# Linear attention, SwiGLU and a bilinear layer in one kernel: attention's stores move to ScalarE's queue, four weight tiles are staged whole, and the gated product stays in PSUM

## The chip, the cores and the metric

The kernel runs on one core of a Trainium2 chip. The metric is the device time of one execution in microseconds; the number of a kernel is the median of its runs. Besides, one execution is profiled, and all durations below come from it.

## What is computed

Three layers in fp32, each feeding the next. Attention works on 4 batches with 8 heads, 576 positions and a head dimension of 64; the other two layers work on its 4 * 576 = 2304 tokens, with a model width of 512 and a hidden width of 1536:

```
q_s = exp(q - max over d);   q_s = q_s / (sum over d + 1e-9)
k_s = exp(k - max over s);   k_s = k_s / (sum over s + 1e-9)
x   = q_s @ (k_s^T @ v)                    per batch and head
x   = (silu(x @ w_gate) * (x @ w_val)) @ moe_w_out
out = ((x @ w_a) * (x @ w_b)) @ moe2_w_out
```

## The kernel before, in words

**Tokens and weights.** The tokens are cut into five token tiles: 512 positions of each of the four batches, and a last tile of 256 columns with the 64 positions that remain of each batch. The hidden width is cut into 12 weight tiles of 128 (f = 0 to 11). A weight tile holds its share of the three matrices of a layer, and each matrix twice: as a high part in fp32r and as what remains (the low part). A product of two fp32 numbers is made of three matmuls with these parts, so a token tile of 512 columns takes 12 matmuls for the gate, 12 for the value and 12 for the down product in each weight tile. The products of layer 0 go through the token tiles 0, 1, 2, the tile of the remainders, and 3 (`order`), then layer 1 goes through all five.

**Conversion of the weights** (`convert`, L308 to 374; `split`, L292 to 294). The raw halves of a weight tile are loaded in three DMAs of 256 KB (L331, L336) into a staging buffer `raw`. ScalarE takes the absolute value (L353; VectorE can do it at L355), scales the raw low words (L357), VectorE clamps, shifts and joins (L359, L362, L365), GpSimd adds (L370), ScalarE copies the high part into the weight tile (L293), and VectorE or GpSimd subtracts it to get the low part (`pair`, L287). Layer 0's weight tiles are converted while token tile 0 goes through them, layer 1's later. The staging buffers are `wr0` and `wr1`, and for the first ten tiles of layer 0 also `xraw`. Tile 0 is converted matrix by matrix, the others in two halves of all three matrices (`convert_tile`, L376). Each weight tile has its own place `w0` to `w11` in SBUF, which layer 0 and layer 1 share. The places `w8` to `w11` serve first as working memory of attention's units of batches 0 and 1.

**Attention** (`attend`) works in units of two heads, four units to a batch. The remainders' positions of batch 0 come in six loads of 64 KB (`load_rests`, L385). A unit ends with two products: 512 columns (`xt`, L589) and the 64 remaining ones (`xl`, L599). Batch 0's `xt` is split at once into the input of token tile 0 (`xhl`); of the other batches ScalarE copies it to `xs` (L596), and SyncE's queue stores it to a DRAM tensor `x` (L597). The remainders are copied to `xq` (L603) and stored (L604) for every batch. A later token tile is loaded from that tensor (`next_x`, L614).

**Gate and value** (`ups`, `gated`, `down`). Two PSUM banks, `gv0` and `gv1`, take the gate's and the value's products; either may go into either. ScalarE applies silu (layer 1: a copy) from the gate's bank to `s` in SBUF (L665), VectorE multiplies `s` by the value's bank into `s` (L668), ScalarE copies the high part to `h` (L293), and VectorE or GpSimd subtracts it from `s` to get h's low part (L287). The down product of tile f comes after the gate and value products of tile f + 1.

**What orders the work.** A planner (`Plan`) gets every operation with its engine, an estimated cost, the buffers that it reads and writes, and, for the products, a due time. `prepare` hands due times back from consumers to producers. `order` then simulates the engines and each time takes the ready operation that is due first on the engine that is free first; it also picks the place of each buffer that may have several, and the engine where there is a choice. A VectorE operation marked `port` and a GpSimd operation are never planned at the same time. `emit` issues the operations in that order, and each engine executes its own in order. Every load of weights and of q, k and v is chained to the one before (`load`, L303), so they issue on SyncE's queue in the order of the program; stores stand on the same queue. The planner reckons a DMA at a start of 1.1 us, an end of 0.95 us and `DMA_RATE` bytes per us.

Of the kernel before, what the change touches and what calls it, by code (L numbers as in the profile page):

```python
# [30 lines left out]
class Plan:  # L31
# [12 lines left out]
    DMA_START, DMA_END, DMA_RATE = 1.1, 0.95, 360e3  # L44
# [50 lines left out]
    def prepare(self):  # L95

        ops = self.ops
        self.succ = [[] for _ in ops]
        for n, op in enumerate(ops):
            for d in op["deps"] | op["order"]:  # L100
                self.succ[d].append(n)
        self.due = [0.0] * len(ops)
        for n in reversed(range(len(ops))):
            op = ops[n]
            cost = op["cost"]
            if op["engine"] == "sync":
                cost += self.DMA_START + self.DMA_END + op["nbytes"] / self.DMA_RATE
            t = self.FAR
            for s in self.succ[n]:
                hop = self.hop(op["engine"], ops[s]["engine"], self.SLACK) if n in ops[s]["deps"] else 0.0  # L110
                t = min(t, self.due[s] - hop)
            t -= cost
            self.due[n] = t if op["wanted"] is None else min(t, op["wanted"])

    def order(self):
# [34 lines left out]
        while len(done) < len(ops):  # L150
# [30 lines left out]
            if engine == "sync":  # L181
# [30 lines left out]
def kernel(  # L212
# [64 lines left out]
    def pool_us(n, streams=2):  # L277
        return (0, 0.14 + n / 1100, 0.15 + n / 449, 0.18 + n / 590)[streams]
# [17 lines left out]
    def dma(fn, nbytes, reads, writes, due=None, after=(), issue=0.475):  # L296
        return add("sync", issue, fn, reads, writes, due=due, nbytes=nbytes, after=after)
# [12 lines left out]
    RAW = WR + ("xraw",)  # L310
    TOP = 122880.0
    LEAST = 2.0 ** -15

    def convert(l, f, c, ms, c0, c1, spare):
# [4 lines left out]
        raw = Buf(sp, [P, n, width, 2], U32, RAW if spare else WR, f"wr{name}")  # L319
# [5 lines left out]
        parts = [(raw, x) for x in range(n)]  # L325
        for x, m in enumerate(ms):
            w_parts[l, f][m].append(c)

            def get(x=x, m=m):
                if m < 2:  # L330
                    nc.sync.dma_start(  # L331
                        out=raw()[:, x].rearrange("p (c n) t -> p c (n t)", n=P),
                        in_=mats[l][m][:, f * 2 * P:(f + 1) * 2 * P].rearrange(
                            "(c p) n -> p c n", p=P)[:, c0 // P:c1 // P, :])
                else:
                    nc.sync.dma_start(  # L336
                        out=raw()[:, x].rearrange("p n t -> p (n t)"),
                        in_=mats[l][m][f * P:(f + 1) * P, 2 * c0:2 * c1])

            load(get, P * width * 8, [(raw, x)])  # L340

        def low():
            return raw()[:, :, :, 0]

        def high():
            return raw()[:, :, :, 1]

        def part(t):
# [9 lines left out]
            out=low(), in_=low(), func=AF.Copy, scale=2.0 ** -29), parts, [(raw, "low")])  # L358
# [13 lines left out]
        add("gpsimd", pool_us(e), lambda: whole(nc.gpsimd), [a, (raw, "low")], [a],  # L372
# [3 lines left out]
    def convert_tile(l, f):  # L376
        for h in range(2):
            spare = l == 0 and f < NF - 2
            list(convert(l, f, h, [0, 1, 2], h * WC // 2, (h + 1) * WC // 2, spare))
# [5 lines left out]
    def load_rests(b, src, at):  # L385

        for h in range(HG):
            load(lambda h=h: nc.sync.dma_start(
                out=rests()[rest(h), at],
                in_=src[b, :, SM:S, :].rearrange("(g h) s d -> h s g d", h=HG)[h]),  # L390
                SL * KD * D * 8, [(rests, (at, h))], issue=0.65)

    def attend(b, g, xhl, due):
# [200 lines left out]
        else:  # L594
            ob = Buf(op, [P, 512], F32, ("ob0", "ob1"), f"xs{u}")
            add("scalar", act_us(SM), lambda: nc.scalar.copy(out=ob(), in_=px()), [px], [ob])  # L596
            dma(lambda: nc.sync.dma_start(out=xd[0][b]()[:, g, :], in_=ob()), P * SM * 4,  # L597
                [ob], [(xd[0][b], g)])
# [5 lines left out]
        dma(lambda: nc.sync.dma_start(out=xd[0][B]()[:, g, b * SL:(b + 1) * SL], in_=oc()[:, 0:SL]),  # L604
            P * SL * 8, [oc], [(xd[0][B], (g, b))])
# [55 lines left out]
    def gated(l, i, f, ga, gb):  # L661
# [7 lines left out]
            out=s()[:, 0:n], in0=s()[:, 0:n], in1=gb()[:, 0:n], op=ALU.mult), [s, gb], [s])  # L669
        split(lambda: h()[:, 0, 0:n], lambda: h()[:, 1, 0:n], lambda: s()[:, 0:n], n, (h, 0), (h, 1), s)  # L670
# [132 lines left out]
```

## Time and profile before

| | |
|---|---|
| median of 3 runs | 1038.8 us (1037.66 to 1039.71) |
| the profiled execution | 1037.9 us |
| its span, first to last instruction | 1036.0 us |
| TensorE busy (matmuls) | 977.9 us, 94% of the span |
| VectorE busy | 431.8 us, 42% |
| ScalarE busy | 357.7 us, 35% |
| GpSimd busy | 178.2 us, 17% |
| moved by DMA | 74.22 MB |

In the profile PE is TensorE's matmuls and PEld its weight loads, DVE is VectorE, ACT is ScalarE, POOL is GpSimd, SP is SyncE and SPq its queue of DMA issues. A time in a row counts from the start of the span. In a timeline a row has the start, the duration, the engine, the line, the operation and the tiles written and read; in brackets stands how long the engine was idle before it and what ended that. An operation's line can be that of a helper: L287 is every difference of a high and a low part and some of attention's, L293 every copy of a high part, so the tiles tell which it is.

### The profile page before, as it was taken

To read this page: it belongs to the slowest core of one execution; us is meant where nothing else is said; L and a number is where in the kernel's file an instruction comes from. 1 tells how busy PE (TensorE), PEld (TensorE's weight loads), DVE (VectorE), ACT (ScalarE), POOL (GpSimd) and SP (SyncE) were. 2 spreads that over 40 slices of the span, in tenths; PEclk is the share of its full clock that TensorE was granted. 3 is DMA by queue.
4 is the path that set the end of the run, shared out by engine and by line. 5 is a ranking of instruction groups with operands and counts; after the bars stand their busy time and mean duration, and the time that the engine had idled before them with its cause. 6 is when DMAs were issued, how large, how long until landed. Compare 5 with 4: busy or idle time off the path is not lost.

```text
span 1036.0 us, 12377 instructions
## 1 busy us (share of the span) xinstructions
PE 977.9 (94%) x4792; PEld 797.4 (77%) x4792; DVE 431.8 (42%) x758; ACT 357.7 (35%) x574; POOL 178.2 (17%) x156
## 2 busy tenths in 40 slices
PE   4777879999999999999999999999999999999997
PEld 3455656677778777799888788888888888888897
DVE  5876688633334333432665774131113112111211
ACT  4556565432334323422355543121112112111211
POOL 4543444301110101100145443000000000000000
PEclk9989989999999999999999999999999999999999
DMA  6445543311121111521133531020002000100100
GB/s 198 120 134 168 168 149 111 117 56 47 47 69 59 46 46 46 175 92 61 62 123 122 194 108 54 1 82 1 1 1 82 1 1 0 61 1 1 41 1 22
DMA packets 63876, 74.22 MB, mean 72 GB/s; under 512 B 12616, under 2 KB 51016, under 8 KB 62920
## 3 DMA queue, kind: packets, MB, share of 16 engines
q1 hardware_dynamic: 63816, 73.42, 22.4%
q8 instruction: 38, 0.62, 0.3%
q14 instruction: 22, 0.18, 0.1%
HBM read 60.29 MB, written 13.11 MB: 71 GB/s over the span
## 4 chain that ended last, share of the span: by engine, by line
PE 80%; DMA 6%; DVE 5%; SPq 3%; issue 2%; ACT 2%; POOL 2%; DVEq 0%; POOLq 0%; ACTq 0%
PE u L654 51%; PE acc L684 14%; PE acc L681 11%; DMA wr<-in_moe_w_out_dram 3%; PE kv L544 2%; POOL a L370 1%; DVE a L365 1%; SPq L331 1%; DVE h L287 1%; SPq L461 1%; PE xt L589 1%; PE kv L546 1%; PE qt L574 1%; DMA ut<-in_v_dram 1%; DMA x<-ob 1%
## 5 line engine op out<-in xcount | busy, mean ns | idle before, releaser
L654 PE MATMUL u<-xhl,w 128*128 128x512 f32 (+1 forms) x2856 | 621.9, 372 | 14.8 <-DVE w L287 12.6
L654 PEld LDWEIGHTS u<-xhl,w 128*128 128x128 f32 x2856 | 497.0, 189 | 110.6 <-DVE w L287 11.7
L668 DVE TENSOR_TENSOR s<-s,u 128x512 f32<-128x512 f32 (+1 forms) x120 | 76.1, 634 | 395.1 <-PE u L654 382.7
L681 PE MATMUL acc<-h,w 128*128 128x512 f32 (+1 forms) x720 | 167.6, 379 | 12.5 <-DVE h L287 10.7
L681 PEld LDWEIGHTS acc<-h,w 128*128 128x128 f32 x720 | 125.5, 190 | 42.3 <-DVE h L287 14.4
L684 PE MATMUL acc<-w,h 128*128 128x512 f32 x648 | 157.5, 391 | 0.1
L665 ACT ACTIVATE s<-u 128x512 f32<-128x512 f32 (+1 forms) x120 | 66.6, 555 | 262.0 <-PE u L654 255.2
L684 PEld LDWEIGHTS acc<-w,h 128*128 128x128 f32 x648 | 120.7, 188 | 26.2 <-DVE h L287 1.3
L293 ACT CAST h<-s 128x512 fp32r<-128x512 f32 (+1 forms) x120 | 69.1, 576 | 205.0 <-DVE s L668 204.7
L370 POOL TENSOR_TENSOR a<-a,wr 128x768 uint32<-128x768 uint32 (+1 forms) x49 | 99.4, 2033 | 205.0 <-DVE a L365 141.4
L287 DVE TENSOR_TENSOR h<-s,h 128x512 fp32r<-128x512 f32 (+1 forms) x119 | 84.3, 709 | 51.5 <-ACT h L293 51.3
L287 POOL TENSOR_TENSOR xhl<-xraw,xhl 128x512 fp32r<-128x512 f32 (+1 forms) x5 | 6.0, 1202 | 337.9 <-ACT xhl L293 240.9
L365 DVE SCALAR_TENSOR_TENSOR a<-wr,a 128x768 uint32<-128x768 uint32 (+1 forms) x49 | 52.4, 1077 | 0.5
L353 ACT ACTIVATE a<-wr 128x768 f32<-128x768 f32 (+1 forms) x38 | 33.7, 888 | 45.0 <-DMA wr<-in_moe_w_out_dram 34.9
L293 ACT CAST w<-a 128x768 fp32r<-128x768 f32 (+1 forms) x49 | 39.9, 818 | 23.2 <-POOL a L370 19.8
L357 ACT ACTIVATE wr<-wr 128x768 uint32<-128x768 uint32 (+1 forms) x49 | 43.8, 893 | 10.3 <-DMA wr<-in_moe_w_out_dram 10.3
L359 DVE TENSOR_SCALAR a<-a 128x768 f32<-128x768 f32 (+1 forms) x49 | 36.0, 739 | 18.8 <-ACT a L353 18.3
L287 DVE TENSOR_TENSOR w<-a,w 128x768 fp32r<-128x768 f32 (+1 forms) x38 | 38.3, 1021 | 8.5 <-ACT w L293 8.5
L567 POOL TENSOR_TENSOR ua<-ua,st 128x576 f32<-128x576 f32 x8 | 9.2, 1154 | 122.4 <-DVE st L566 122.4
L362 DVE TENSOR_SCALAR a<-a 128x768 uint32<-128x768 uint32 (+1 forms) x49 | 27.6, 572 | 0.8
L287 POOL TENSOR_TENSOR w<-a,w 128x768 fp32r<-128x768 f32 (+1 forms) x11 | 22.9, 2080 | 19.6 <-ACT w L293 19.6
L697 DVE COPY ob<-acc 128x512 f32<-128x512 f32 (+1 forms) x20 | 12.7, 636 | 27.9 <-DMA out_dram<-ob 19.9
(94 smaller groups left out, 439.2 us busy)
## 6 DMA issues: line engine op xcount, KB each, us to landing
wr<-in_moe_w_out_dram SPq DMA_DIRECT2D x46, 256.0 KB
xraw<-x SPq DMA_DIRECT2D x7, 1024.0 KB
wr<-in_moe_w_a_dram SPq DMA_DIRECT2D x24, 256.0 KB
wr<-in_moe_w_b_dram SPq DMA_DIRECT2D x24, 256.0 KB
wr<-in_moe_w_gate_dram SPq DMA_DIRECT2D x22, 256.0 KB
wr<-in_moe_w_val_dram SPq DMA_DIRECT2D x22, 256.0 KB
x<-ob SPq DMA_DIRECT2D x16, 256.0 KB
out_dram<-ob SPq DMA_DIRECT2D x16, 256.0 KB
```

What stands on the lines that cost most here:

```text
L287: engine.tensor_tensor(out=out(), in0=x(), in1=y(), op=op)
L293: add("scalar", act_us(n), lambda: nc.scalar.copy(out=hi(), in_=src()), [src_key], [hi_key])
L353: add("scalar", act_us(e) + 0.08, lambda: nc.scalar.activation(out=a().bitcast(F32), in_=high().bitcast(F32), func=AF.Abs), parts, [a], ot ...
L357: add("scalar", act_us(e) + 0.08, lambda: nc.scalar.activation(out=low(), in_=low(), func=AF.Copy, scale=2.0 ** -29), parts, [(raw, "low")])
L359: add("vector", dve_us(e, 2), lambda: nc.vector.tensor_scalar(out=a().bitcast(F32), in0=a().bitcast(F32), scalar1=TOP, scalar2=LEAST, op0= ...
L365: add("vector", dve_us(e), lambda: nc.vector.scalar_tensor_tensor(out=a(), in0=high(), scalar=0xC0000000, in1=a(), op0=ALU.bitwise_and, op ...
L370: engine.tensor_tensor(out=a(), in0=a(), in1=low(), op=ALU.add)
L654: nc.tensor.matmul(ps()[:, 0:n], lhsT=wv[:, c, :], rhs=x()[:, xs, c, 0:n], start=(a == 0 and c == 0), stop=(a == 2 and c == KD - 1))
L665: add("scalar", act_us(n), lambda: nc.scalar.activation(out=s()[:, 0:n], in_=ga()[:, 0:n], func=AF.Silu if l == 0 else AF.Copy), [ga], [s] ...
L668: add("vector", dve_us(n), lambda: nc.vector.tensor_tensor(out=s()[:, 0:n], in0=s()[:, 0:n], in1=gb()[:, 0:n], op=ALU.mult), [s, gb], [s])
L681: nc.tensor.matmul(ps()[:, 0:n], lhsT=w()[:, 4 + ws, o * P:(o + 1) * P], rhs=h()[:, hs, 0:n], start=begin, stop=end)
L684: nc.tensor.matmul(ps(), lhsT=h()[:, hs, o * P:(o + 1) * P], rhs=w()[:, 4 + ws, :], start=begin, stop=end)
```

## The change

The stores of `xs` and `xq` and the six loads of the remainders are issued from ScalarE's queue; the loads of the remainders leave the chain of loads. The raw words of layer 0's weight tiles 1 to 4 are staged whole, in the places `w4` to `w7`, which are not yet in use as weight tiles then; tile 0 and tiles 5 to 11 keep the small staging buffers. The multiplication of the gate writes its result into the value's PSUM bank and not into `s`, and both steps of the split read it there; the subtraction can no longer go to GpSimd and is not marked `port`. The planner reckons 300e3 bytes per us where it had 360e3, and takes an operation as a DMA by its bytes, not by its engine.

```diff
@@ -41,7 +41,7 @@
...
-    DMA_START, DMA_END, DMA_RATE = 1.1, 0.95, 360e3
+    DMA_START, DMA_END, DMA_RATE = 1.1, 0.95, 300e3
@@ -103,7 +103,7 @@
...
-            if op["engine"] == "sync":
+            if op["nbytes"]:
@@ -178,7 +178,7 @@
...
-            if engine == "sync":
+            if op["nbytes"]:
@@ -293,8 +293,8 @@
...
-    def dma(fn, nbytes, reads, writes, due=None, after=(), issue=0.475):
-        return add("sync", issue, fn, reads, writes, due=due, nbytes=nbytes, after=after)
+    def dma(fn, nbytes, reads, writes, due=None, after=(), issue=0.475, queue="sync"):
+        return add(queue, issue, fn, reads, writes, due=due, nbytes=nbytes, after=after)
@@ -308,42 +308,47 @@
...
+    AHEAD = 4
...
-    def convert(l, f, c, ms, c0, c1, spare):
+    def convert(l, f, c, ms, c0, c1, spare, raw=None):
...
-        raw = Buf(sp, [P, n, width, 2], U32, RAW if spare else WR, f"wr{name}")
+        if raw is None:
+            raw, rows, h = Buf(sp, [P, n, width, 2], U32, RAW if spare else WR, f"wr{name}"), (lambda: raw()), 0
+        else:
+            rows, h = (lambda: raw()[:, c]), c
...
-        parts = [(raw, x) for x in range(n)]
+        parts = [(raw, (h, x)) for x in range(n)]
...
             def get(x=x, m=m):
...
-                        out=raw()[:, x].rearrange("p (c n) t -> p c (n t)", n=P),
+                        out=rows()[:, x].rearrange("p (c n) t -> p c (n t)", n=P),
...
-                        out=raw()[:, x].rearrange("p n t -> p (n t)"),
+                        out=rows()[:, x].rearrange("p n t -> p (n t)"),
...
-            load(get, P * width * 8, [(raw, x)])
+            load(get, P * width * 8, [(raw, (h, x))])
         def low():
-            return raw()[:, :, :, 0]
+            return rows()[:, :, :, 0]
         def high():
-            return raw()[:, :, :, 1]
+            return rows()[:, :, :, 1]
@@ -355,7 +360,7 @@
...
-            out=low(), in_=low(), func=AF.Copy, scale=2.0 ** -29), parts, [(raw, "low")])
+            out=low(), in_=low(), func=AF.Copy, scale=2.0 ** -29), parts, [(raw, (h, "low"))])
@@ -369,14 +374,16 @@
         def whole(engine):
...
-        add("gpsimd", pool_us(e), lambda: whole(nc.gpsimd), [a, (raw, "low")], [a],
+        add("gpsimd", pool_us(e), lambda: whole(nc.gpsimd), [a, (raw, (h, "low"))], [a],
...
     def convert_tile(l, f):
+        spare, raw = l == 0 and f < NF - 2, None
+        if l == 0 and f <= AHEAD:
+            raw = Buf(wp, [P, 2, 3, WC // 2, 2], U32, f"w{f + NF - KD - AHEAD - 1}", f"wr{l}_{f}")
...
-            spare = l == 0 and f < NF - 2
-            list(convert(l, f, h, [0, 1, 2], h * WC // 2, (h + 1) * WC // 2, spare))
+            list(convert(l, f, h, [0, 1, 2], h * WC // 2, (h + 1) * WC // 2, spare, raw))
@@ -385,10 +392,10 @@
     def load_rests(b, src, at):
...
-            load(lambda h=h: nc.sync.dma_start(
+            dma(lambda h=h: nc.scalar.dma_start(
...
-                SL * KD * D * 8, [(rests, (at, h))], issue=0.65)
+                SL * KD * D * 8, [], [(rests, (at, h))], issue=0.65, queue="scalar")
@@ -594,15 +601,15 @@
...
-            dma(lambda: nc.sync.dma_start(out=xd[0][b]()[:, g, :], in_=ob()), P * SM * 4,
-                [ob], [(xd[0][b], g)])
+            dma(lambda: nc.scalar.dma_start(out=xd[0][b]()[:, g, :], in_=ob()), P * SM * 4,
+                [ob], [(xd[0][b], g)], queue="scalar")
...
-        dma(lambda: nc.sync.dma_start(out=xd[0][B]()[:, g, b * SL:(b + 1) * SL], in_=oc()[:, 0:SL]),
-            P * SL * 8, [oc], [(xd[0][B], (g, b))])
+        dma(lambda: nc.scalar.dma_start(out=xd[0][B]()[:, g, b * SL:(b + 1) * SL], in_=oc()[:, 0:SL]),
+            P * SL * 8, [oc], [(xd[0][B], (g, b))], queue="scalar")
@@ -666,8 +673,8 @@
...
-            out=s()[:, 0:n], in0=s()[:, 0:n], in1=gb()[:, 0:n], op=ALU.mult), [s, gb], [s])
-        split(lambda: h()[:, 0, 0:n], lambda: h()[:, 1, 0:n], lambda: s()[:, 0:n], n, (h, 0), (h, 1), s)
+            out=gb()[:, 0:n], in0=s()[:, 0:n], in1=gb()[:, 0:n], op=ALU.mult), [s, gb], [gb])
+        split(lambda: h()[:, 0, 0:n], lambda: h()[:, 1, 0:n], lambda: gb()[:, 0:n], n, (h, 0), (h, 1), gb, psum=True)
```

## Rows read from the trace of the kernel before

**Rows 1.** The stretches, 45 to 400 us: busy us (and instructions) of each engine, granted clock, DMA share, GB/s.

```profile
45.00:100.00 55.00, 41.03 (x174) 30.50 (x174) 41.33 (x67) 35.98 (x50) 23.49 (x18) 0.90 0.54 168
100.00:200.00 100.00, 85.95 (x393) 63.40 (x392) 77.42 (x128) 55.67 (x80) 41.44 (x31) 0.96 0.42 133
200.00:400.00 200.00, 200.00 (x985) 158.32 (x985) 70.37 (x164) 69.48 (x110) 18.06 (x33) 1.00 0.18 55
```

**Rows 2.** Groups by line, 45 to 200 us: busy us, mean ns | idle before, its releaser.

```profile
L287 DVE TENSOR_TENSOR h<-s,h 128x512 fp32r<-128x512 f32 x11 | 10.4, 942 | 0.7 <-ACT h L293 0.7
```

**Rows 3.** Instructions on tile h, 690 to 980 us: min/median/max ns, first and last start.

```profile
L287 DVE TENSOR_TENSOR h<-s,h x36: 692/693/1428, 692.4 to 975.5; 128x512 fp32r<-128x512 f32 x36
```

**Rows 4.** Waits of TensorE, 0 to 200 us: total us, times, longest.

```profile
PE u L654 <- DVE w L287: 12.6, 5, 7.5
PE acc L681 <- DVE h L287: 9.2, 5, 6.0
PE xt L589 <- ACT ut L583: 6.6, 4, 2.9
```

**Rows 5.** Timeline around 41 us.

```profile
41.23 0.89 ACT L353 ACTIVATE a<-wr 128x768 f32<-128x768 f32 x1 [4.26 <-DMA wr<-in_moe_w_out_dram]
...
43.17 1.96 PE L589 MATMUL xt<-ut 128*128 128x512 f32 x2 [2.77 <-ACT ut L583]
```

**Rows 6.** Timeline, 52 to 71 us.

```profile
52.53 1.83 POOL L370 TENSOR_TENSOR a<-a,wr 128x768 uint32<-128x768 uint32 x1 [0.72 <-DVE a L365]
...
56.46 0.69 DVE L519 TENSOR_REDUCE st<-ut 128x8 f32<-128x512 f32 x1 [3.42 <-DMA ut<-in_q_dram]
...
70.59 0.56 DVE L355 TENSOR_SCALAR a<-wr 128x768 uint32<-128x768 uint32 x1 [1.11 <-DMA wr<-in_moe_w_out_dram]
```

**Rows 7.** Waits of SyncE's queue, 100 to 130 us.

```profile
SPq L597 <- ACT xq L603: 6.0, 1, 6.0
```

**Rows 8.** Timeline, 122 to 132 us.

```profile
122.04 0.40 SPq L331 DMA_DIRECT2D wr<-in_moe_w_gate_dram  x1
...
127.84 0.89 ACT L353 ACTIVATE a<-wr 128x768 f32<-128x768 f32 x1 [4.66 <-DMA wr<-in_moe_w_out_dram]
...
128.76 0.56 DVE L359 TENSOR_SCALAR a<-a 128x768 f32<-128x768 f32 x1 [3.88 <-ACT a L353]
...
131.34 4.30 POOL L370 TENSOR_TENSOR a<-a,wr 128x768 uint32<-128x768 uint32 x2 [9.59 <-issue]
```

**Rows 9.** Instructions on tiles xs and xq, 45 to 200 us: min/median/max ns of an issue.

```profile
L597 SPq DMA_DIRECT2D x<-xs x4: 339/354/433, 87.5 to 183.7; - x4
...
L604 SPq DMA_DIRECT2D x<-xq x5: 338/377/2167, 59.6 to 186.4; - x5
```

**Rows 10.** Timeline of the opening.

```profile
2.27 1.41 SPq L388 DMA_DIRECT2D rests<-in_k_dram  x2
...
6.33 1.26 SPq L388 DMA_DIRECT2D rests<-in_v_dram  x2
...
9.04 0.66 ACT L353 ACTIVATE a<-wr 128x512 f32<-128x512 f32 x1 [7.02 <-DMA wr<-in_moe_w_gate_dram]
```

**Rows 11.** The chain that ended last, in order of time: start us, us, what.

```profile
9.47 6.12 DMA ut<-in_v_dram
```

**Rows 12.** The stretch 10 to 20 us, columns as in rows 1.

```profile
10.00:20.00 10.00, 4.18 (x25) 3.19 (x26) 6.99 (x22) 6.53 (x15) 4.27 (x7) 1.00 0.90 306
```

**Rows 13.** Line 668 in the whole span: min/median/max ns.

```profile
L668 DVE TENSOR_TENSOR s<-s,u x120: 414/689/690, 52.4 to 1027.7; 128x512 f32<-128x512 f32 x96, 128x256 f32<-128x256 f32 x24
```

**Rows 14.** Timeline in the full stretch, 693 to 697 us.

```profile
693.21 0.60 ACT L665 ACTIVATE s<-u 128x512 f32<-128x512 f32 x1 [0.82 <-DVE h L287]
...
695.30 0.69 DVE L668 TENSOR_TENSOR s<-s,u 128x512 f32<-128x512 f32 x1 [2.19 <-PE u L654]
...
696.68 0.69 DVE L287 TENSOR_TENSOR h<-s,h 128x512 fp32r<-128x512 f32 x1 [0.69 <-ACT h L293]
```

**Rows 15.** The chain that ended last, behind it.

```profile
697.95 5.44 PE u L654 x24
```

## The prediction, made before the changed kernel was built or run

> **What bounds the kernel now.** I read the stretches of the span first, then who TensorE waits for, then the timeline around the waits. The stretches [rows 1] show two regimes. From 200 us TensorE is busy all the time (200.00 of 200); an edit elsewhere can win nothing there unless it takes work from TensorE, and this change takes none. Before 200 us it is not: 41.03 of the 55 from 45 to 100, 85.95 of the next 100. That is most of the first pass over token tile 0, in which the weights are converted as they are used. In those 155 us (45 to 200) VectorE is busy 41.33 + 77.42 = 118.8 and GpSimd 23.49 + 41.44 = 64.9. Together that is more than 155, so the two must overlap, and GpSimd's sums and VectorE's two-input operations visibly get in each other's way: the first pass's subtraction for h takes 942 ns on average [rows 2], against a median of 693 late in the run, where GpSimd has little to do [rows 3]. So the first pass hangs on the conversion chain (load, ScalarE, VectorE, GpSimd, ScalarE, VectorE). TensorE's waits before 200 us [rows 4] agree: 12.6 us for converted weights, 9.2 us for the low half of h, which stands in VectorE's queue among conversions, 6.6 us for a ScalarE copy of attention. What a part of the change is worth is the idle time that it takes out of this chain; whatever ends the first pass earlier moves all that follows earlier by as much.
>
> **Tiles 1 to 4 staged whole.** The 24 loads of these tiles no longer wait for one of three small buffers, so they can issue right behind the opening loads. Three idle times before 100 us end with a load. (a) ScalarE stands 4.26 us for tile 1's first half, with attention's transposed q queued behind it, and TensorE waits 2.77 us for that copy [rows 5]. With tile 1 landed long before, the copy comes that much earlier: I take 2.8, between 0 (another conversion takes ScalarE's slot) and 4.3. (b) VectorE waits 3.42 us for batch 1's q, until 56.46 [rows 6]; GpSimd had stopped at 52.53 + 1.83 = 54.36, so both stood for 2.1. Those loads sit in SP's queue behind weight loads that waited for a buffer. I take 2.1, between 0 and 3.4. (c) VectorE waits 1.11 for weights at 70.59 [rows 6]: 1.1, between 0 and 1.1. Together **6.0, between 0 and 8.8**. What is late next is VectorE itself: TensorE's 12.6 us for weights are mostly its work and not the loads', so I count nothing more for them. From tile 5 on the ring has three buffers as before.
>
> **Attention's stores on ScalarE's queue.** SP works in order, and a store that waits for attention holds the weight loads behind it. The clear case: SP waits 6.0 us at the store of xs [rows 7]; the weights behind it issue at 122.04, ScalarE stands 4.66 us for them, VectorE 3.88, GpSimd has been idle for 9.59 by 131.34 [rows 8]. With the store gone the load could issue up to 6.0 us earlier, more than ScalarE waits. I take VectorE's **3.9, between 0 and 6.0**. In the later passes SP's waits for stores cost nothing, since TensorE is full there; that cover is gone only if x of the next tile came late.
> The price is ScalarE's: a store issues in 0.35 us (xs) or 0.38 (xq) at the median, 0.43 at most where it did not wait [rows 9]. Between 45 and 200 us there are nine such stores (four xs, five xq), 9 x 0.43 = 3.9 us at most, on an engine that is busy 35.98 + 55.67 = 91.7 of 155. Behind a store on ScalarE stand conversions and the activation; most stores fall into idle time, so I take **1.0 lost, between 0 and 3.9**. No row shows a DMA issued from ScalarE; SP's are the nearest. The six loads of the remainders issue on ScalarE before its first work at 9.04, for which it idles 7.02 today [rows 10]: nothing.
>
> **The opening.** Three pairs of remainder loads leave SP's queue, from 1.41 us for the first pair to 1.26 for the last [rows 10], 3.9 in all. The first v load issues at 9.47 and takes 6.12 to land, on the chain of waits [rows 11]. It can issue 3.9 earlier, but the DMA engines then are 0.90 busy at 306 GB/s [rows 12], and the same bytes lie ahead of it. I take **1.5, between 0 and 3.9**, nearer the low end as that row is the nearest. [...]
>
> **The gated product in PSUM.** The three steps stay the same in number. The subtraction now has one operand in PSUM. The multiplication, which has that form today, never took over 690 ns in 120 executions, beside GpSimd or not [rows 13]. So 11 subtractions go from 942 to 693 [rows 2, 3]: 11 x 0.249 = **2.7 won**, between 1.0 lost and 8.3 won (twelve times 0.69, if GpSimd runs on beneath all of them). One more that GpSimd did goes to VectorE, within that bound. No row shows VectorE writing to PSUM; the loss end allows 0.08 on each of twelve multiplications. [...]
> What it adds is a longer hold: the value product's bank is free after the subtraction, not after the multiplication. In the full stretch the subtraction ends 2.07 us after the multiplication starts [rows 14], while the next value product comes after 12 or 24 matmuls at 5.44 / 24 each [rows 15], 2.72 or 5.44 us: covered. In the first pass subtractions are late, and TensorE already waited five times for one [rows 4]. The next value product can then take the gate's bank instead, once the activation (0.60) [rows 14] has read it; that costs about 0.7 each time. I take **1.2 lost, between 0 and 3.5** (five times 0.7). What is freed sooner is s, so the next activation starts earlier.
>
> **The planner.** The new DMA rate and due times re-sort each engine's order. This has no row; I add nothing, and 4 us either way for it, from the size of the single stalls above (2.8 to 3.9).
>
> **The sum.** 6.0 + 3.9 + 1.5 + 2.7 - 1.0 - 1.2 = 11.9. The profiled execution took 1037.9 us, of which the span is 1036.0 and 1.9 lies around it: 1037.9 - 11.9 = 1026.0. The median of the runs, 1038.8, is 0.9 above it, so I forecast 1026.9.
>
> **Rivals.**
> *Hidden anyway.* The loads come early, but batch 1's attention loads stand between tile 2's and tile 3's on the same queue and wait there for the slot of a batch 0 unit, and VectorE with GpSimd has no less to do. For it speaks that the two are nearly full; against it that (b) and the 3.9 are idle time of both. Then 1.5 of the load terms is left: 1.5 + 2.7 - 2.2 = 2.0, or 1036.8. Chance 0.18.
> *Slower: the held bank.* The plan's due times know that a subtraction is wanted by the down product, not that the bank is wanted one product sooner. If plan and chip disagree over which bank is free first, TensorE stands before the value product, and 12 matmuls (2.72 us) that used to run meanwhile come after. It decides from the fifth such pass (5 x 2.72 = 13.6 against 13.1 won); at eight of the twelve it gives 21.8 - 13.1 = 8.7 more: 1047.5. For it speaks TensorE's 9.2 us for h, against it the gate's bank and the full stretch. Chance 0.14.
> *Larger.* With weights always there, TensorE's waits for w and h both go: 12.6 + 9.2 = 21.8, or 1017. The granted clock, 0.90 between 45 and 100 us, would then rise too. Against it: VectorE's work stays. Chance 0.14.
> The forecast has the rest, 0.54, with an own range of 1019 to 1034.
>
> **How the numbers follow.** A measurement here tells 0.2% (2.1 us) from no change. Faster: nearly all of the forecast, half of "hidden anyway", all of "larger": 0.76. Same: the other half, 0.08. Slower: the bank, and a little of a bad re-sorting: 0.16. The range goes from 1013, below "larger" by the planner's 4, to 1041, just over today's time; it leaves out the held bank and a sliver below.
>
> **What would show it.** In the changed kernel's timeline: ScalarE's wait before tile 1's conversion and VectorE's for batch 1's q gone; no store among SP's issues before 200 us, and no common idle time of VectorE and GpSimd of about 4 us in the second half of the first pass; the subtraction near 0.69 in the first pass; the first pass ending some 12 us earlier, with TensorE full behind it. Wrong it would be if TensorE waits before the value product's matmuls for the subtraction, if ScalarE's new issues show up as waits of VectorE or TensorE, if the first pass ends where it did, or if the stretch after it grows.

## The result, and the profile after

The changed kernel takes 1022.11 us at the median (four runs, 1020.18 to 1022.68) where the kernel before took 1039.26 beside it on the same chip (1037.66 to 1041.15): a ratio of 0.9831, interval 0.981 to 0.9852, so 17.1 us less. The forecast was 1026.9. The profiled execution took 1021.98 us with a span of 1020.2, against 1037.9 and 1036.0.

**Where the time came from.** The stretches of the changed kernel answer to [rows 1]; columns as there.

```profile
45.00:100.00 55.00, 47.03 (x211) 34.92 (x211) 50.53 (x79) 35.55 (x49) 32.05 (x20) 0.94 0.27 81
100.00:200.00 100.00, 91.37 (x434) 69.78 (x435) 73.04 (x124) 60.55 (x88) 35.63 (x27) 0.95 0.43 136
200.00:400.00 200.00, 200.00 (x972) 159.00 (x970) 69.96 (x164) 67.57 (x110) 18.96 (x35) 1.00 0.17 51
```

Between 45 and 100 us TensorE gets 6.0 us more done, VectorE 9.2 and GpSimd 8.6: the waits between them shrank. From 200 us TensorE is full, as before. The end of the first pass, which is the end of the last down product of token tile 0, can be read off TensorE's timeline in both kernels. First the kernel before:

```profile
198.33 2.56 PE L681 MATMUL acc<-h,w 128*128 128x512 f32 x10 [0.65 <-DVE h L287]
```

Then rows of the changed kernel's timeline: a part of the opening, a subtraction in the first pass, the place where TensorE waits for a held bank, and the end of the pass.

```profile
4.59 2.80 ACTq L395 DMA_DIRECT2D rests<-in_v_dram  x2
6.27 0.37 SPq L468 DMA_DIRECT2D ut<-in_q_dram  x1
...
8.91 0.37 SPq L336 DMA_DIRECT2D wr<-in_moe_w_val_dram  x1
...
9.32 0.51 SPq L468 DMA_DIRECT2D ut<-in_v_dram  x1
...
42.06 1.14 PE L646 MATMUL u<-xhl,w 128*128 128x512 f32 x3
...
64.39 1.86 POOL L375 TENSOR_TENSOR a<-a,wr 128x768 uint32<-128x768 uint32 x1
...
65.04 0.69 DVE L287 TENSOR_TENSOR h<-u,h 128x512 fp32r<-128x512 f32 x1 [0.66 <-ACT h L293]
...
116.14 0.68 DVE L287 TENSOR_TENSOR h<-u,h 128x512 fp32r<-128x512 f32 x1
...
116.87 3.01 PE L661 MATMUL u<-xhl,w 128*128 128x512 f32 x12 [1.02 <-DVE h L287]
...
182.50 3.01 PE L688 MATMUL acc<-h,w 128*128 128x512 f32 x12
```

The first pass ended at 198.33 + 2.56 = 200.9 and now ends at 182.50 + 3.01 = 185.5. These 15.4 us are nearly the whole 15.8 by which the spans differ; what follows takes as long as it did (1036.0 - 200.9 = 835.1 us before, 1020.2 - 185.5 = 834.7 now). They arise although the pass begins later: the first gate product starts at 42.06, where it started at 38.37.

Who TensorE waits for up to 200 us, in the changed kernel (total us, times, longest), beside [rows 4]:

```profile
PE u L661 <- DVE w L287: 7.3, 6, 4.1
PE kx L505 <- DVE km L287: 7.2, 2, 6.6
PE kv L551 <- ACT ut L541: 6.1, 2, 5.3
...
PE u L661 <- DVE h L287: 1.0, 1, 1.0
```

The 12.6 us for converted weights are 7.3, and the 9.2 for the low half of h before the down product are gone. The 6.6 for attention's copies to xt are gone too, but TensorE's four largest waits in attention's products still sum to 21.6 us: before it was 8.0 (kx), 6.6 (xt), 5.2 and 1.8 (kv), now it is 7.2 (kx), 6.1 and 4.9 (kv), 3.4 (qt). So the gain lies in the waits for weights and for h. In this plan the held bank costs the one wait of 1.0.

### The profile page after: what moved, and what is told of

Same layout as the page of the kernel before. It is cut to its first block, busy times and chain, and to the rows that moved or that the text cites. A ratio compares the mean times of both kernels' runs of the same rounds, so it can differ in the third digit from the quotient of the medians.

```text
span 1020.2 us, 12311 instructions
## 1 busy us (share of the span) xinstructions
PE 977.8 (96%) x4792; PEld 800.5 (78%) x4792; DVE 426.9 (42%) x755; ACT 354.6 (35%) x577; POOL 177.1 (17%) x156
## 4 chain that ended last, share of the span: by engine, by line
PE 86%; DMA 4%; DVE 4%; ACT 2%; issue 1%; POOL 1%; SPq 1%; ACTq 0%; POOLq 0%; DVEq 0%
PE u L661 54%; PE acc L691 14%; PE acc L688 12%; DMA wr<-in_moe_w_out_dram 2%; PE kv L551 2%; PE xt L596 1%; DMA wr<-in_moe_w_val_dram 1%; POOL a L375 1%; DVE a L370 1%; PE kv L553 1%; DVE a L367 1%; DMA x<-xq 1%; DMA rests<-in_q_dram 1%; PE qt L581 1%; SPq L336 1%
## 5 line engine op out<-in xcount | busy, mean ns | idle before, releaser
L675 DVE TENSOR_TENSOR u<-s,u 128x512 f32<-128x512 f32 (+1 forms) x120 | 77.1, 643 | 408.7 <-PE u L661 389.4
L688 PE MATMUL acc<-h,w 128*128 128x512 f32 (+1 forms) x720 | 162.8, 374 | 0.3 <-DVE h L287 0.2
L293 ACT CAST h<-u 128x512 fp32r<-128x512 f32 (+1 forms) x120 | 65.1, 543 | 210.7 <-DVE u L675 210.7
L287 DVE TENSOR_TENSOR h<-u,h 128x512 fp32r<-128x512 f32 (+1 forms) x120 | 76.3, 636 | 49.1 <-ACT h L293 48.8
L370 DVE SCALAR_TENSOR_TENSOR a<-wr,a 128x768 uint32<-128x768 uint32 (+1 forms) x49 | 57.1, 1174 | 0.7
L358 ACT ACTIVATE a<-wr 128x768 f32<-128x768 f32 (+1 forms) x41 | 36.3, 890 | 26.0 <-DMA wr<-in_moe_w_out_dram 22.2
L364 DVE TENSOR_SCALAR a<-a 128x768 f32<-128x768 f32 (+1 forms) x49 | 32.4, 670 | 23.8 <-ACT a L358 23.6
L287 DVE TENSOR_TENSOR w<-a,w 128x768 fp32r<-128x768 f32 x37 | 38.6, 1051 | 5.9 <-ACT w L293 5.6
L287 POOL TENSOR_TENSOR w<-a,w 128x768 fp32r<-128x768 f32 (+1 forms) x12 | 21.5, 1796 | 26.1 <-ACT w L293 21.6
```

What stands on the lines that cost most here:

```text
L287: engine.tensor_tensor(out=out(), in0=x(), in1=y(), op=op)
L293: add("scalar", act_us(n), lambda: nc.scalar.copy(out=hi(), in_=src()), [src_key], [hi_key])
L358: add("scalar", act_us(e) + 0.08, lambda: nc.scalar.activation(out=a().bitcast(F32), in_=high().bitcast(F32), func=AF.Abs), parts, [a], ot ...
L370: add("vector", dve_us(e), lambda: nc.vector.scalar_tensor_tensor(out=a(), in0=high(), scalar=0xC0000000, in1=a(), op0=ALU.bitwise_and, op ...
L675: add("vector", dve_us(n), lambda: nc.vector.tensor_tensor(out=gb()[:, 0:n], in0=s()[:, 0:n], in1=gb()[:, 0:n], op=ALU.mult), [s, gb], [gb])
L688: nc.tensor.matmul(ps()[:, 0:n], lhsT=w()[:, 4 + ws, o * P:(o + 1) * P], rhs=h()[:, hs, 0:n], start=begin, stop=end)
```

## The experiments

Two readings of the gain stood against each other: that loads and stores act **on the chip**, by the idle times that the prediction lists, or that the **plan**, which sorts every engine anew at any edit, does it. So the parts were tried alone and left out with a new plan each, and then two of them without a new plan, in the old order. All ratios are to the kernel before on the same chip (1038.61 us beside the first four, 1039.23 beside the others). The table's last two columns are from TensorE's timeline in each profiled execution: the start of the first gate product and the end of the first pass (start plus duration of its last row). They come from one execution each, and single executions differ: the ten runs of u6_port took 1030.06 to 1036.87 us and its profiled one 1036.81, the four of u4_psum took 1024.76 to 1029.90 and its profiled one 1024.76. Differences of 2 or 3 us in the last column are therefore not safe by themselves; the ratios stand beside them.

| run | what | ratio (interval) | first product, us | pass ends, us |
|---|---|---|---|---|
| before | | 1 | 38.4 | 200.9 |
| p1_rate | DMA rate of the planner alone | 0.998 (0.996 to 1.0) | 36.3 | 197.8 |
| p2_stores | ScalarE's queue alone | 0.9942 (0.992 to 0.9965) | 35.1 | 196.0 |
| p3_staged | staging alone | 0.9929 (0.9901 to 0.9956) | 42.3 | 194.5 |
| p4_psum | product in PSUM alone | 0.9916 (0.9891 to 0.9941) | 38.4 | 194.7 |
| u3_staged | changed, without staging | 0.9891 (0.986 to 0.9923) | 43.4 | 190.8 |
| u4_psum | changed, product in s | 0.9883 (0.9855 to 0.9912) | 42.8 | 188.6 |
| u6_port | changed, other plan | 0.9939 (0.992 to 0.9958) | 43.1 | 198.6 |
| q2_spstores | changed, SyncE issues the stores | 0.9845 (0.9823 to 0.9867) | 43.4 | 187.0 |
| q3_actstores | old order, ScalarE issues | 0.9951 (0.9934 to 0.9969) | 37.4 | 197.2 |
| q4_staged | old order, tiles 1 to 4 staged | 0.9923 (0.9894 to 0.9951) | 38.8 | 194.5 |
| q6_both | old order, both | 0.9911 (0.9888 to 0.9934) | 37.7 | 192.9 |
| n1_low_later | changed, scaling later | 0.9902 (0.9866 to 0.9938) | 45.4 | 190.8 |
| the change | | 0.9831 (0.981 to 0.9852) | 42.1 | 185.5 |

### Each part alone, with a new plan

p1_rate, the planner's DMA rate:

```diff
-    DMA_START, DMA_END, DMA_RATE = 1.1, 0.95, 360e3
+    DMA_START, DMA_END, DMA_RATE = 1.1, 0.95, 300e3
```

> The kernel before with the planner's DMA rate at 300e3 and nothing else. Theory (the loads' waits leave the first pass): within 0.4% of before, 1035 to 1043 us, because no wait is taken away. Rival 'the new order': the gain lies in the re-sorting by the new rate, and this run alone is at 1030 us or lower.

p2_stores, the stores of xs and xq and the loads of the remainders on ScalarE's queue, with the planner's two lines that tell a DMA by its bytes:

```diff
-            dma(lambda: nc.sync.dma_start(out=xd[0][b]()[:, g, :], in_=ob()), P * SM * 4,
-                [ob], [(xd[0][b], g)])
+            dma(lambda: nc.scalar.dma_start(out=xd[0][b]()[:, g, :], in_=ob()), P * SM * 4,
+                [ob], [(xd[0][b], g)], queue="scalar")
...
```

> The kernel before with the stores of xs and xq and the six remainder loads on ScalarE's queue. Theory: 3.9 from the weight loads that stood behind a store, 1.5 in the opening, 1.0 lost on ScalarE: about 4 us faster than before, 1033 to 1036 us. Rival 'the DMA engines are the limit, not the queue': within 1 us of before.

p3_staged, the whole buffers for tiles 1 to 4:

```diff
+        if l == 0 and f <= AHEAD:
+            raw = Buf(wp, [P, 2, 3, WC // 2, 2], U32, f"w{f + NF - KD - AHEAD - 1}", f"wr{l}_{f}")
...
```

> The kernel before with tiles 1 to 4 staged whole. Theory: the largest part, about 6 us faster than before, 1031 to 1035 us, TensorE's 2.8 us wait for attention's copy near 41 us and VectorE's 3.4 us wait for batch 1's q gone. Rival 'hidden anyway' (VectorE and GpSimd have no less to do): at most 2 us faster, 1037 us or more.

p4_psum, the product in the value's bank:

```diff
-            out=s()[:, 0:n], in0=s()[:, 0:n], in1=gb()[:, 0:n], op=ALU.mult), [s, gb], [s])
+            out=gb()[:, 0:n], in0=s()[:, 0:n], in1=gb()[:, 0:n], op=ALU.mult), [s, gb], [gb])
...
```

> The kernel before with the gated product in PSUM. Theory: the subtraction near 690 ns instead of 942, some 2.7 us won and 1.2 lost by the held bank: 1.5 us faster, 1036 to 1039 us. Rival 'held bank': slower than before, with waits of TensorE before the value product. Rival 'this is the largest part' (low half of h no longer late, 9.2 us of TensorE's waits): 1031 us or lower.

Measured: the rate alone 0.2% (its interval reaches to no change), the queue 6 us (0.0058 x 1039), staging 7.4, the product 8.7. The parts add up to 24 us with the rate's 2, the change gives 17.1, so they take some of the same idle time, or owe a part to their plans. The product in PSUM gives most, where the prediction had 1.5 net. But each of these has a new order as well, so none is yet the price of its edit.

### One part taken out of the change, with a new plan

u3_staged (the ring's three buffers for all tiles) and u4_psum (product and split in s again):

```diff
-        if l == 0 and f <= AHEAD:
+        if False:
```

> The changed kernel with tiles 1 to 4 back in the small staging buffers. If the parts each took out idle time of their own, about 6 us are lost: 1027 to 1030 us. Rival 'the parts overlap' (alone they gave 2.5, 5.9, 6.6 and 8.5 us, 23.5 together, where the change gave some 17): 3 us or less are lost, 1025 us or lower.

```diff
-            out=gb()[:, 0:n], in0=s()[:, 0:n], in1=gb()[:, 0:n], op=ALU.mult), [s, gb], [gb])
-        split(lambda: h()[:, 0, 0:n], lambda: h()[:, 1, 0:n], lambda: gb()[:, 0:n], n, (h, 0), (h, 1), gb, psum=True)
+            out=s()[:, 0:n], in0=s()[:, 0:n], in1=gb()[:, 0:n], op=ALU.mult), [s, gb], [s])
+        split(lambda: h()[:, 0, 0:n], lambda: h()[:, 1, 0:n], lambda: s()[:, 0:n], n, (h, 0), (h, 1), s)
```

> The changed kernel with the gated product back in s in SBUF. Theory 'the product in PSUM is the largest part' (alone 8.5 us): 1028 to 1032 us, with subtractions held up again and TensorE waiting for h's low half at the down product. Rival 'the parts overlap': 1025 us or lower.

Without staging the kernel takes 1028.55 us, without the PSUM product 1026.65: 6.4 and 4.5 above the change, the second between its two expectations. What the product does on the chip is seen on tile h in the first pass. These are its subtractions in u4_psum, up to 200 us (min, median and max ns):

```profile
L287 DVE TENSOR_TENSOR h<-s,h x11: 673/683/2332, 64.2 to 196.9; 128x512 fp32r<-128x512 f32 x11
```

And in the changed kernel, up to 190 us:

```profile
L287 DVE TENSOR_TENSOR h<-u,h x12: 676/688/693, 58.2 to 181.3; 128x512 fp32r<-128x512 f32 x12
```

With two operands in SBUF the longest takes 2.33 us; the longest of the kernel before took 1.92, and its mean was 942 ns [rows 2]. With one operand in PSUM none takes over 0.693, and the row at 65.04 above lies wholly within a sum of GpSimd (64.39 to 66.25). In the kernel before the same pair looks like this:

```profile
76.11 4.79 POOL L370 TENSOR_TENSOR a<-a,wr 128x768 uint32<-128x768 uint32 x2 [0.94 <-DVE a L365]
...
77.26 1.92 DVE L287 TENSOR_TENSOR h<-s,h 128x512 fp32r<-128x512 f32 x1
```

### The same operations in another plan

u6_port marks the subtraction of h in the plan as one that must not run beside GpSimd, as it was before. The chip gets the changed kernel's operations, with the product in PSUM; the order differs, and with it the engine of a few operations that two engines can do (up to 200 us GpSimd does four subtractions for the weights where it did three, and ScalarE 22 absolute values where it did 23).

```diff
-        pair(n, lo, src, lambda: hi().bitcast(F32), ALU.subtract, [src_key, hi_key], [lo_key], not psum, not psum)
+        pair(n, lo, src, lambda: hi().bitcast(F32), ALU.subtract, [src_key, hi_key], [lo_key], not psum, not psum or src_key.tag == ("gv0", "gv1"))
```

> The changed kernel, but the planner again never puts the subtraction for h beside a GpSimd operation; the instructions are the same, only their order can differ. If the gain of the product in PSUM comes from the chip (an operand that no GpSimd operation holds up), the time stays within 0.3% of the changed kernel, 1019 to 1025 us. Rival 'it comes from the plan' (the subtraction may be placed beside GpSimd): most of the gain is lost, 1028 us or more.

It takes 1033.35 us, 11 more than the change, and in the profiled execution, one of its slowest, the first pass ends 13.0 us later. Waits of VectorE and TensorE up to 200 us show where it stands (total us, times, longest):

```profile
DVE u L675 <- PE u L661: 19.2, 7, 6.8
PE u L661 <- ACT s L672: 5.3, 7, 1.8
PE u L661 <- DVE h L287: 1.9, 1, 1.9
...
PE acc L688 <- DVE h L287: 1.0, 1, 1.0
```

In the changed kernel VectorE waits 2.9 us for a product of TensorE in this way, in three waits. In u6_port it is put to wait for it, with conversions behind it. TensorE waits there for the activation that has to read a bank, seven times and 5.3 us in all (0.76 each; in the changed kernel once, 0.6), which is near the 0.7 each that the prediction gave a held bank. A part is TensorE's clock: between 150 and 200 us the granted clock was 0.93 in u6_port and 1.00 in the change, and after a wait for weights 22 matmuls took 7.81 us (185.06) where the change's took 5.32 (174.51). So a plan can cost 11 us, for one mark in the planner.

q2_spstores leaves plan and order of the change as they are, and lets SyncE issue the stores of xs and xq. The six loads of the remainders stay on ScalarE's queue, other than its expectation says:

```diff
-            dma(lambda: nc.scalar.dma_start(out=xd[0][b]()[:, g, :], in_=ob()), P * SM * 4,
+            dma(lambda: nc.sync.dma_start(out=xd[0][b]()[:, g, :], in_=ob()), P * SM * 4,
...
```

> The changed kernel's plan and order on TensorE, VectorE and GpSimd, but the stores and remainder loads issued by SyncE at the same places of the order. Theory: SyncE's loads stand behind stores again, so about 4 us are lost, 1025 to 1028 us. Rival 'with tiles 1 to 4 staged the loads come early enough anyway': within 1.5 us of the changed kernel.

1023.0 us: 0.9 above the change, and the intervals of the two overlap. In this plan, a store that stands in SyncE's queue holds up little.

### The old order, with the loads and stores moved

Here no plan is made anew. The planner works on the kernel before, and only what the chip does with its order is changed. q3_actstores lets ScalarE issue the stores and the loads of the remainders; q4_staged gives each half of tiles 1 to 4 its place in w4 to w7 after the plan is made; q6_both does both.

```diff
-            dma(lambda: nc.sync.dma_start(out=xd[0][b]()[:, g, :], in_=ob()), P * SM * 4,
+            dma(lambda: nc.scalar.dma_start(out=xd[0][b]()[:, g, :], in_=ob()), P * SM * 4,
...
```

> The kernel before with its own plan and its own order on every engine; only the engine that issues the stores of xs and xq and the six loads of the remainders is now ScalarE. Against the run with the same edit and a new plan (6.5 us faster than before) it separates the queue from the plan. If the queue does it on the chip: the 6.0 us that SP stands at a store and the 3.9 us of idle VectorE behind it go, 3 to 6 us faster (ratio 0.994 to 0.997). If the plan does it: within 1 us of before (0.999 to 1.001).

```diff
     def __call__(self):
+        if self.view:
+            return self.view()
...
+        if l == 0 and 1 <= f <= 4:
+            if f not in big:
+                big[f] = Buf(wp, [P, 2, 3, WC // 2, 2], U32, f"w{f + NF - KD - 5}", f"wr{l}_{f}")
+            raw.view = lambda: big[f]()[:, c]
```

> The kernel before with its own plan and its own order on every engine; only the place of the loads of tiles 1 to 4 is changed: each goes into its own part of the empty buffer of a later tile's weights and so waits for no conversion. Against the run with staging and a new plan (7.2 us faster than before) it separates the earlier loads from the plan. If the prediction's terms (a) to (c) hold: 4 to 7 us faster (0.993 to 0.996), ScalarE's 4.26 us wait at 41 us and VectorE's 3.42 us for batch 1's q gone. If the plan does it: 0 to 2 us faster (0.998 to 1.000), with the waits gone but the first pass ending where it did.

> The two edits before this together (ScalarE issues stores and remainder loads; tiles 1 to 4 have places of their own), still in the order of the kernel before. If loads and stores act on the chip by themselves: the sum of the two, 7 to 12 us faster (0.988 to 0.993). If they remove the same wait, no more than the larger one. If the order does it: 0 to 3 us faster (0.997 to 1.000); then what is left of the 16.5 us is the plan's.

q3_actstores is 5.1 us faster (0.0049 x 1039), and in its profile the first pass ends 3.7 earlier. Its timeline at the place of [rows 8], with TensorE's down products ahead of it and behind it:

```profile
117.40 0.37 SPq L331 DMA_DIRECT2D wr<-in_moe_w_gate_dram  x1
...
120.31 2.96 PE L681 MATMUL acc<-h,w 128*128 128x512 f32 x12
...
123.61 0.92 ACT L353 ACTIVATE a<-wr 128x768 f32<-128x768 f32 x1 [0.72 <-DVE w L287]
...
127.16 4.36 POOL L370 TENSOR_TENSOR a<-a,wr 128x768 uint32<-128x768 uint32 x2 [6.47 <-DMA wr<-in_moe_w_out_dram]
...
132.68 0.79 PE L681 MATMUL acc<-h,w 128*128 128x512 f32 x1 [3.32 <-DVE h L287]
```

The same operations of the kernel before, where [rows 8] does not have them:

```profile
121.70 2.96 PE L681 MATMUL acc<-h,w 128*128 128x512 f32 x12
...
136.81 0.80 PE L681 MATMUL acc<-h,w 128*128 128x512 f32 x1 [5.96 <-DVE h L287]
```

The load issues at 117.40, not 122.04; ScalarE's conversion starts at 123.61, not 127.84, and no longer waits for a load; GpSimd's sum starts at 127.16, not 131.34. This is the mechanism of the prediction, at the place that it named. TensorE was 1.4 us ahead before it (121.70 - 120.31) and is 4.1 ahead behind it (136.81 - 132.68), so the store is worth 2.7 there; 1.0 came from the opening, in which the first product starts that much earlier.

q4_staged is 8.0 us faster, above the 4 to 7 expected, and its first pass ends 6.4 earlier. Its timeline at the places of [rows 5, 6] and on to the subtraction at 130 us:

```profile
38.78 0.90 ACT L359 ACTIVATE a<-wr 128x768 f32<-128x768 f32 x1 [1.38 <-POOL w L289]
...
50.56 0.60 ACT L671 ACTIVATE s<-u 128x512 f32<-128x512 f32 x1 [0.63 <-PE u L645]
...
52.29 0.68 DVE L525 TENSOR_REDUCE st<-ut 128x8 f32<-128x512 f32 x1
...
64.09 2.96 PE L687 MATMUL acc<-h,w 128*128 128x512 f32 x12
...
68.01 0.90 SPq L337 DMA_DIRECT2D wr<-in_moe_w_gate_dram  x1
...
83.05 0.94 ACT L359 ACTIVATE a<-wr 128x768 f32<-128x768 f32 x1
...
86.00 3.18 PE L687 MATMUL acc<-h,w 128*128 128x512 f32 x12
...
115.70 2.96 PE L687 MATMUL acc<-h,w 128*128 128x512 f32 x12
...
130.69 0.80 PE L687 MATMUL acc<-h,w 128*128 128x512 f32 x1 [5.99 <-DVE h L289]
...
191.95 2.54 PE L687 MATMUL acc<-h,w 128*128 128x512 f32 x10 [0.67 <-DVE h L289]
```

And the same operations of the kernel before:

```profile
50.63 0.60 ACT L665 ACTIVATE s<-u 128x512 f32<-128x512 f32 x1
...
67.11 3.18 PE L681 MATMUL acc<-h,w 128*128 128x512 f32 x12
...
85.18 0.87 SPq L331 DMA_DIRECT2D wr<-in_moe_w_gate_dram  x1
...
89.35 0.63 PE L681 MATMUL acc<-h,w 128*128 128x512 f32 x2
...
91.17 0.91 ACT L353 ACTIVATE a<-wr 128x768 f32<-128x768 f32 x1 [2.36 <-DMA wr<-in_moe_w_out_dram]
```

Tile 1's conversion starts at 38.78, not 41.23, and no longer behind a DMA, but the first activation behind it starts at 50.56, where it did at 50.63: that gain is gone by then. Batch 1's q is reduced at 52.29, not 56.46, without a wait, and the down product behind it starts 3.0 us earlier (67.11 - 64.09). For the product at 86.00 it is 3.35 us (89.35 before). For the one at 115.70 it is 6.0 (121.70 before): ScalarE no longer waits 2.36 us for the weights that it converts at 91.17 (now 83.05). They are the first half of tile 5, which is not staged itself; its loads issue at 68.01 and not at 85.18, with tiles 1 to 4 out of the ring's buffers. The prediction has no term for tile 5. TensorE's waits for weights up to 200 us go from 12.6 to 7.6 us. What is late next is the subtraction of h: TensorE still waits 5.99 us for it at 130.69.

q6_both is 9.2 us faster (0.0089 x 1039), and the first pass ends 8.0 earlier, where the single edits sum to 3.7 + 6.4 = 10.1 (by the ratios 5.1 + 8.0 = 13.1). So loads and stores act on the chip in the old order, and together they give less than their sum: once the tiles are staged, the stores' move moves the pass's end by 194.5 - 192.9 = 1.6. The stall itself is no smaller with the tiles staged. In q4_staged SyncE still stands at the store (its queue's wait between 60 and 200 us: total us, times, longest), and ScalarE behind it:

```profile
SPq L603 <- ACT xs L602: 6.3, 1, 6.3
```

```profile
121.70 0.90 ACT L359 ACTIVATE a<-wr 128x768 f32<-128x768 f32 x1 [4.47 <-DMA wr<-in_moe_w_out_dram]
```

In q6_both the same conversion starts at 117.22 without a wait, and TensorE gains by it:

```profile
117.22 0.89 ACT L359 ACTIVATE a<-wr 128x768 f32<-128x768 f32 x1
...
126.83 0.50 PE L687 MATMUL acc<-h,w 128*128 128x512 f32 x1 [1.39 <-DVE h L289]
```

The down product is 3.9 us ahead of q4_staged's there (130.69 - 126.83), but the next one, at 141.66 against 143.25, only 1.6. What is missing from the sum is lost behind the stall, between 130 and 143 us.

### An attempt to go further

The first product of the changed kernel starts 3.7 us later than before, while ScalarE scales staged halves early (at 27.73, 30.21, 32.32 and 36.34, 0.9 us each), ahead of attention's work. n1_low_later orders that scaling after the absolute value of the same half.

```diff
-        add("scalar", act_us(e) + 0.08, lambda: nc.scalar.activation(
+        first = add("scalar", act_us(e) + 0.08, lambda: nc.scalar.activation(
...
-            out=low(), in_=low(), func=AF.Copy, scale=2.0 ** -29), parts, [(raw, (h, "low"))])
+            out=low(), in_=low(), func=AF.Copy, scale=2.0 ** -29), parts, [(raw, (h, "low"))], after=(first,))
```

> The changed kernel with one order added to the plan: ScalarE's scaling of a half's low words comes after the same half's absolute value, so that with the loads landed early it no longer stands ahead of attention's exponentials (four of them, 0.91 us each, lay between 27 and 37 us, and the first u product came 3.7 us later than before). If these hold the first product back: it starts 2 to 4 us earlier and the kernel is 1 to 4 us faster than the change (1018 to 1021, ratio 0.980 to 0.983). If VectorE and GpSimd bound the first pass anyway, or the plan sorts worse: within 2 us of the change or slower (1021 to 1026).

A miss: 1029.9 us, 7.8 above the change, and the first product starts at 45.4, later still. The scaling is gone from that stretch, but ScalarE then stands for VectorE:

```profile
38.45 1.16 ACT L541 ACTIVATE ut<-ut 128x1152 f32<-128x1152 f32 x1 [3.25 <-DVE ut L287]
```

So without the early scaling the first product comes no sooner; what the scaling itself costs isn't shown, since n1_low_later is a new plan too. In the old order the product starts at 37.7 with the tiles staged and ScalarE issuing (q6_both), so the later start goes with the new plan. It does not decide the end: u3_staged, u4_psum and the change all start at 42 to 43 and end far earlier than the kernel before. No run beat the change.

## Why the prediction was right, and where it was off

The direction, the range and the place (all of it in the first pass) came out; the forecast was 4.8 us too slow. In the profiled executions the pass ends 15.4 us earlier where the sum had 11.9. The terms, each by its run's first pass, and by the ratios of the table above (x 1039):

| term | predicted, us | first pass, us | by ratio, us | from |
|---|---|---|---|---|
| staged loads | 6.0 | 6.4 | 8.0 | q4_staged: 200.9 - 194.5 |
| stores, ScalarE's issues, opening | 3.9 - 1.0 + 1.5 = 4.4 | 3.7 | 5.1 | q3_actstores: 200.9 - 197.2 |
| what the two lose together | 0 | -2.1 | -3.8 | q6_both: 8.0 - 10.1 |
| the planner | 0, 4 either way | 4.3 | 2.9 | u4_psum against q6_both: 192.9 - 188.6 |
| PSUM product less the held bank, with its order | 2.7 - 1.2 = 1.5 | 3.1 | 5.4 | the change against u4_psum: 188.6 - 185.5 |
| sum | 11.9 | 15.4 | 17.6 | |

In the last two terms the columns differ because u4_psum's profiled execution was the fastest of its four. The intervals of u4_psum and q6_both overlap, so the planner's row is not told from nothing.

**Staged loads: right in sum, partly by luck.** The waits of (a) and (b) are gone as said. But (a), 2.8 us in the sum, gave nothing that lasted (50.63 against 50.56); (b), 2.1 in the sum, gave about 3.0; from then on to 89 us, where (c) lies, it was 0.3; and 2.65 came between 89 and 122 us, with tile 5's weights. The step that failed is that the sum ends with tile 4: it puts the tiles from 5 on and TensorE's 12.6 us for weights at nothing, as VectorE's work and not the loads', but with the loads early the 12.6 are 7.6.

**Stores: right in the mechanism, but the gain is not kept.** The stall at [rows 8] is really there, and q3_actstores takes it: VectorE's 3.9 us of idle time are worth 2.7 to TensorE. The step that failed is adding them in full to the staged loads: with the tiles staged the stall is as long as before, its removal puts TensorE 3.9 us ahead, and 2.3 of these are lost again behind it, so that 1.6 stay. Why they are lost was not looked into. ScalarE's price was small: four issues of xs take 326 to 390 ns and six of xq 326 to 397 in the changed kernel between 45 and 200 us, and none appears among the waits shown.

**The opening: near in size, wrong as a step.** The first v load was to issue up to 3.9 us earlier; it issues at 9.32 where it did at 9.47 [rows 11], and at 9.55 in q3_actstores. SyncE's waits up to 14 us in the changed kernel say why (total us, times, longest):

```profile
SPq L336 <- DMA wr<-in_moe_w_gate_dram: 2.3, 1, 2.3
SPq L468 <- DMA rests<-in_k_dram: 1.7, 1, 1.7
```

The load at 8.91, right ahead of the v load, waits until the first gate weights have landed. In the kernel before SyncE waited 0.3 us for that; the issues of the remainders filled the time. So here a wait for a landing took the place of what left the queue. The prediction looked at the issues and not at what the issue behind them waits for. In the old order ScalarE's first copy of v still starts 1.2 us sooner, at 14.42 (q3_actstores) and not at 15.62, where it had waited 2.52 us for the load: the v load lands sooner, though it issues no sooner. The first product gained 1.0 us by it (37.4 against 38.4); in the changed kernel it comes later. Of the 3.9 us of issues 0.15 was saved for the v load (9.47 - 9.32).

**The PSUM product: right in kind, at half its size or less.** The subtractions went from 942 ns to 0.69 us, as from [rows 2, 3]: no cost of a PSUM source shows (median 688 ns in the pass, 683 with two SBUF operands in u4_psum). The 0.08 us that the loss end allowed on a multiplication that writes to PSUM came from no row; measured is 0.011 (median 697 ns in the pass of the changed kernel, 686 with the result in SBUF before). What the sum lacked are TensorE's waits for h before the down product (9.2 us, [rows 4]): in the change they are gone, and u4_psum still has five, of 6.8 us together. That the subtraction may now stand in the plan beside GpSimd does not explain it alone: in u6_port it may not, and one wait of 1.0 us is left there too. How the gain divides between the chip's shorter subtractions and the new order stays open and wasn't tried: there is no run with the product in PSUM in the old order, nor with the product in SBUF in the new one.

**The held bank: came as sized in this plan.** TensorE waited once, 1.0 us, against 1.2 predicted. The rival that ends slower needed 2.72 us at five places or more. In u6_port the bank costs more (5.3 us in seven waits and 1.9 in one), so its price is the plan's to set.

**The planner: the term that was undersized.** 4 us either way came from the length of single stalls. The same operations in two plans took times 11 us apart (u6_port), and one more ordering edge cost 7.8 us in all (n1_low_later). What the table has for the planner (4.3 or 2.9) is therefore one draw and not the price of an edit; nor are the gains of p1_rate to p4_psum, which hold a draw each.

**The rivals.** "Hidden anyway" (1036.8) fell with q4_staged and q3_actstores. "Larger" (1017) is nearer than its chance of 0.14 suggests: of the 21.8 us that it took for TensorE's waits, 9.2 + 12.6 - 7.3 = 14.5 went. The granted clock between 45 and 100 us rose, as it said, from 0.90 to 0.94; but between 20 and 45 us it fell, from 0.97 to 0.80.

## What to carry to other kernels

Where one pass is bound by a chain over several engines and the rest is full, price an edit by the idle time at the places it touches, but follow the gain to the end of the pass: here 3.9 us won at a stall were 1.6 at the next down product. Before taking issues off a queue, look what the issue behind them waits for. Where a planner sorts the work anew, keep its order and apply the edit to that order as a control; what remains is the plan's, and it may be as large as the edit. Where a two-input VectorE operation with both operands in SBUF takes longer beneath GpSimd's work (here up to 1.92 us), look whether one operand can stay in PSUM: here the operation kept its 0.69 us.

## What was not expected of the hardware

VectorE's subtraction with both operands in SBUF took 1.92 us beneath GpSimd's sum in the kernel before; with one operand in PSUM it took 0.69 within such a sum, and at most 0.693 in all twelve of the pass.

In the opening, moving three pairs of loads to ScalarE's queue did not bring the first v load forward by more than 0.15 us: SyncE issued nothing for 2.3 us ahead of 8.91, and its waits name the landing of the first gate weights. The row at 4.59 (2.80 us) is no slow issue. It spans two issues with a wait between them, each of 0.602 us:

```profile
L395 ACTq DMA_DIRECT2D rests<-in_v_dram x2: 602/602/602, 4.6 to 6.8; - x2
```
